# Queuing the attention of a chunk two slots later, and copying W's blocks out of PSUM one unit later, in a FAVOR attention and bilinear FFN kernel on Trainium2

## The chip, the cores and the metric

The kernel runs on one core of one Trainium2 chip. Its time is the device time of one execution in microseconds (us), and lower is better. The kernel before took 929.81 us, the median of 3 runs (929.26 to 933.73).

## The reference, cut to what matters

All of it, with the shapes (q, k and v are [8, 8, 576, 64], omega is [128, 64], and the weights are float64):

```python
def phi(x):                                   # x is q or k, divided by 64 ** 0.25
    proj = einsum('bhsd,md->bhsm', x, omega)  # 128 features
    h = proj - sum(x * x, -1, keepdims=True) / 2
    h = h - max(h, -1, keepdims=True)
    return exp(h) / sqrt(128)

q_p, k_p = phi(q), phi(k)
kv  = einsum('bhsm,bhsd->bhmd', k_p, v)
z   = sum(k_p, axis=2)
num = einsum('bhsm,bhmd->bhsd', q_p, kv)
den = einsum('bhsm,bhm->bhs', q_p, z)[..., None] + 1e-06
x   = (num / den).transpose(0, 2, 1, 3).reshape(4608, 512)
out = ((x @ w1) * (x @ w2) @ w3) @ w_out      # w1, w2 [512, 1024], w3 [1024, 1024], w_out [1024, 512]
```

## The kernel before, in words

**The work.** The 4608 tokens are 36 chunks of 128. For each chunk of q and of k the kernel computes features; from k and v it makes kv and z for each of the 8 batches (a batch is 4.5 chunks); a chunk of q then attends, and its result x goes through the bilinear FFN. The last two matrices are multiplied once at the start (W = w3 w_out). Large products run in fp16, each operand as a high and a low part, three passes (PASSES, L25).

**The names.** They are the names of the program's tiles, and the profile's groups use them too.

- *Splits and features.* qraw and kraw are loaded by SyncE (SP); a norm (junk_q on ACT, then a small matmul in power_of_two, L155) gives a scale; qhl and khl are their two parts, the high one by ACT (L136), the low one by DVE (L139). qpj and kpj (L254) are the projections, 24 short matmuls on TensorE (PE) into a pair of PSUM banks; DVE takes the maximum nm (L259) and subtracts it (qe, L267); ACT takes the exponent (L268); eq and ek are the two parts of that, the high one by DVE or ACT (L125, L127), the low one mostly by POOL (L277).
- *Attention.* Two DMA transposes in SP's queue make eqT (L344). nu (L357, in q_attend) is the product with kv, 24 matmuls, into a pair of banks; DVE divides (xs). x_turn (called by ready) splits xs into xhl, and a DMA transposes it into xT (L398).
- *kvp* (L322) is the product of a batch's features with v, one per batch. vhl are the parts of v: of a batch five tiles, the low part of each by DVE at L139.
- *FFN.* A unit of gates (ab, L581) is 48 matmuls of 256 tokens into two single banks; ACT scales one (asb, L590), DVE multiplies with the other (L591), and POOL splits the product (arena, L595 and L596). Two chunks share four units. project_out (o, L607) is 24 matmuls on W for one chunk, an ACT copy and a store.
- *Weights.* Each block of float64 weights goes through from_float64: a fetch by a DMA of ACT's queue (L443), magnitude on ACT (L451) and four bit operations on DVE (bits, L457 to L461). For W a product follows: wp (L530), two single banks, which ACT copies (L535) or DVE adds (L537) into Wb.

**PSUM.** Two pairs of banks (pool ps_a) are used in turn by qpj, kpj, nu and kvp. Four single banks (ps_m) are used in turn by the small norms, wp, the gates, o and the sums of the weights (l1).

**What sets the order.** Each chunk has three slots (PACE). In step, every piece of a chunk is put into a slot with a rank: q's features at its first slot at0, q_attend at at0 + 2, ready at at0 + 3, the k chunk five chunks ahead. The main loop (L748) takes the slots in turn: first some ticks of the weights (PER; a tick holds one stage each of several blocks, set apart by SKEW, L44), then one unit from a queue of gates and project_outs (unit, L637), then the planned pieces by rank. After slot 40 unit leaves two in the queue (RESERVE). A scheduler then orders the instructions of each engine, near to this order but not always in it; an engine runs its own in order, and waits for others by semaphores.

What the change touches: SKEW (L44), features (L245), from_float64's list (L467), W_block (L519), the padding of units (L662), and the two lines of step for q_attend and ready (L724, L725).

Of the kernel before, what the change touches and what calls it, by code (L numbers as in the profile page):

```python
# [7 lines left out]

F32 = mybir.dt.float32
# [4 lines left out]
AF = mybir.ActivationFunctionType  # L14
# [4 lines left out]
P = 128  # L19
# [5 lines left out]
PASSES = ((0, 0), (0, 1), (1, 0))  # L25
# [13 lines left out]
DQ = "10"  # L39
DK = "11111110"  # L40


ORDER = "ooWWWW11a22booWWWW11a22bS"
SKEW = [0, 1, 2, 2, 3]  # L44

PER = [3, 1, 0, 1, 0, 1, 1, 0, 1, 0, 1, 1, 0, 1, 1, 0, 1, 1, 1, 1, 1] + 12 * [1]
PACE = {}
GROUPS = [(0, 1), (1, 1), (2, 1), (3, 1)]
RESERVE = 2
EAGER = 40  # L50
RAW64_BUFS = 3
O_BUFS = 3
RAW_BUFS = 2
# [10 lines left out]
def tile_favor_attention_then_bilinear_ffn(  # L64
# [19 lines left out]
    nc = tc.nc  # L84
    NCH = qT.shape[0]
    H, D = v.shape[2], v.shape[3]
    HD = H * D
    NP = H // 2
    M = omT.shape[1]
# [17 lines left out]
    def banks(name):  # L107
        return ps_a.tile([P, 2, 512], F32, tag="pa", name=name)
# [4 lines left out]
    def small(name, n=1, rows=P, dt=F32, bufs=4):  # L113
        return sm.tile([rows, n], dt, tag=f"s_{name}", name=name, bufs=bufs)

    ones_bf = const.tile([P, P], BF16, name="ones_bf")
    nc.vector.memset(ones_bf, 1.0)
    ones = const.tile([P, P], F32, name="ones")
# [10 lines left out]
    def pick(kinds, i):  # L129
        return kinds[min(i, len(kinds) - 1)]  # L130
# [114 lines left out]
    def features(c, name):  # L245


        hl, es = hls.pop((name, c))
        pj = banks(f"{name}pj_{c}").rearrange("p g (i m) -> p g i m", m=M)
        for i in range(NP):  # L250
            for n, (x, y) in enumerate(PASSES):
                for g in range(2):
                    d = slice(g * D, (g + 1) * D)
                    nc.tensor.matmul(  # L254
                        pj[:, g, i], hl[d, x, i], om[d, y], start=n == 0, stop=n == len(PASSES) - 1
                    )
        pj = pj.rearrange("p g i m -> p (g i) m")
        nm = small("nm", H)
        nc.vector.tensor_reduce(nm, pj, AX.X, ALU.max, negate=True)  # L259
        e = at.tile([P, H, M], F32, tag="e", name=f"{name}e_{c}", bufs=2)  # L260
        if pick(DK if name == "k" else DQ, c) == "1":

            nc.vector.tensor_scalar(nm, nm, es, 15 * math.log(2.0), ALU.mult, ALU.add)
            for h in range(H):
                nc.scalar.activation(e[:, h], pj[:, h], AF.Exp, scale=es, bias=nm[:, h : h + 1])
        else:
            nc.vector.tensor_tensor(e, pj, nm.unsqueeze(2).broadcast_to([P, H, M]), ALU.add)  # L267
            nc.scalar.activation(e, e, AF.Exp, scale=es, bias=ln_e)  # L268
        return e
# [76 lines left out]
    def q_attend(c):  # L346

        t = eqs.pop(c)
        owners = [
            (b, max(b * S - c * P, 0), min((b + 1) * S - c * P, P))  # L350
            for b in range(c * P // S, ((c + 1) * P - 1) // S + 1)
        ]
        nu = banks(f"nu_{c}")[:, :, 0 : 4 * E].rearrange("p g (i e) -> p g i e", e=E)
        for h in range(H):
            for b, r0, r1 in owners:
                for n, (x, y) in enumerate(PASSES):
                    nc.tensor.matmul(  # L357
                        nu[r0:r1, h // 4, h % 4],
                        t[:, x, place(h), r0:r1],
                        kvs[b][:, y, h],  # L360
                        start=n == 0,
                        stop=n == 2,
                    )

        gd = small("gd", H)
        nc.vector.tensor_scalar_add(
            gd.rearrange("p (g i) -> p g i", g=2), nu[:, :, :, D], 1e-6 * M * 2.0**21
        )
        gr = small("gr", H)
        nc.vector.reciprocal(gr, gd)  # L370
        xs = at.tile([P, HD], F32, tag="xs", name=f"xs_{c}", bufs=1)
        nc.vector.tensor_tensor(
            xs.rearrange("p (g i d) -> p g i d", g=2, d=D),
            nu[:, :, :, 0:D],
            gr.rearrange("p (g i) -> p g i", g=2).unsqueeze(3).broadcast_to([P, 2, 4, D]),
            ALU.mult,
        )
        mx = small("mx")
        nc.vector.tensor_reduce(mx, xs, AX.X, ALU.max, apply_absolute_value=True)
        xss[c] = xs, mx, owners  # L380
# [54 lines left out]
    def from_float64(new, src, name):  # L435

        st = {}

        def fetch():
            at = st["at"] = raw_at.pop(0)  # L440
            raw = arena[:, at : at + 4].bitcast(U32).rearrange("p b i -> p (b i)")

            nc.scalar.dma_start(raw.rearrange("p (j i) -> p j i", j=src.shape[1]), src)  # L443
            st["raw"] = raw.rearrange("p (i t) -> p i t", t=2)

        def magnitude():

            at = st["mag"] = mag_at.pop(0)
            st["g"] = arena[:, at : at + 2].rearrange("p b i -> p (b i)")
            st["dst"] = new()  # L450
            nc.scalar.activation(st["g"], st["raw"][:, :, 1].bitcast(F32), AF.Abs)  # L451

        def bits():
            g = st["g"]
            top, low = st["raw"][:, :, 1], st["raw"][:, :, 0]

            nc.vector.tensor_scalar(g, g, F64_TOP, F64_LEAST, ALU.min, ALU.max)  # L457
            g = g.bitcast(U32)
            nc.vector.tensor_scalar(g, g, 3, 0x3FFFFFFF, ALU.logical_shift_left, ALU.bitwise_and)
            nc.vector.scalar_tensor_tensor(g, top, 0xC0000000, g, ALU.bitwise_and, ALU.bitwise_or)  # L460
            nc.vector.scalar_tensor_tensor(  # L461
                st["dst"].bitcast(U32), low, 29, g, ALU.logical_shift_right, ALU.bitwise_or
            )
            raw_at.append(st["at"])
            mag_at.append(st["mag"])

        return [fetch, magnitude, bits, lambda: None]  # L467

    l1s = {}
    done = set()  # L470
# [48 lines left out]
    def W_block(n):  # L519

        i, j0 = n * 2 % NF, n * 2 // NF * HALF
        at = HALF + n % 2 * 2
        w3c = guest[:, at : at + 2].rearrange("p b i -> p (b i)")

        def product():
            w = w3c.rearrange("p (j i) -> p j i", j=HALF)
            for k in range(2):
                ps = bank_m(f"wp_{n}_{k}")
                for j in range(HALF):
                    nc.tensor.matmul(  # L530
                        ps, w[:, j, k * P : (k + 1) * P], guest[:, j], start=j == 0, stop=j == HALF - 1
                    )
                Wi = Wb[:, i + k + 1]
                if j0 == 0:
                    nc.scalar.copy(Wi, ps)  # L535
                else:
                    nc.vector.tensor_tensor(Wi, ps, Wi, ALU.add)  # L537
                    square_sum(wam[:, i + k : i + k + 1], Wi, f"W{i + k}")

        src = w3T[j0 * P : (j0 + HALF) * P, 2 * i * P : 2 * (i + 2) * P]  # L540
        return from_float64(lambda: w3c, src.rearrange("(j p) i -> p j i", p=P), f"w3_{n}") + [product]

    def W_split():
        p, s = power_of_two(wam, NF, "W", add=True, bufs=1)
# [113 lines left out]
    for ch in ORDER:  # L658
        n = seen.get(ch, 0)
        seen[ch] = n + 1  # L660
        st = make[ch](n)
        units.append([None] * 4 + st if len(st) == 1 else st + [None] * (5 - len(st)))  # L662
    behind = sorted(range(5), key=lambda k: -SKEW[k])
    ticks = [
        [units[t - SKEW[k]][k] for k in behind if 0 <= t - SKEW[k] < len(units) and units[t - SKEW[k]][k]]
# [17 lines left out]
    def put(slot, rank, fn):  # L683
        plan.setdefault(slot, []).append((rank, len(plan[slot]) if slot in plan else 0, fn))
# [19 lines left out]
    def step(i):  # L704
        at0 = begin[i]
        kc = i + LEAD
        keys = [(n, c) for n, c in (("q", i), ("k", kc)) if 0 <= c < NCH]
        state = {}

        def norms():  # L710
            state["am"] = norm(keys, i)

        def splits():
            for name, c in keys:
                split_raw(c, name)
                if c + 2 < NCH:
                    load(srcs[name], c + 2, name)

        put(at0 - 3, 3, norms)
        put(at0 - 2, 6, lambda: scale(keys, state["am"]))  # L720
        put(at0 - 1, 8, splits)
        if i >= 0:
            put(at0, 1, lambda: q_chunk(i))
            put(at0 + 2, 7, lambda: q_attend(i))  # L724
            put(at0 + 3, 0, lambda: ready(i))  # L725
        if kc < NCH:
            put(at0, 2, lambda: k_chunk(kc))
        if kc in B_OF_K:

            def kv():  # L730
                v_unit(len(v_work))
                kv_batch(B_OF_K[kc])

            put((begin[i + 1] if i + 1 in begin else at0 + 3) - 1, 5, kv)
        for b in range(B):
            cs = [c for c, _, _ in chunks_of(b)]
            if cs[1] == kc:
                put(at0, 9, lambda b=b: v_batch(b))
            if cs[0] == kc:
                put(at0 + 2, 10, lambda cs=cs: [v_load(c) for c in cs if c not in vraw])  # L740
# [59 lines left out]
```

## Time and profile before

| | before |
|---|---|
| median of 3 runs | 929.81 us |
| the profiled execution | 932.87 us |
| its span, first to last instruction | 931.1 us |
| mean granted clock of TensorE | 0.929 |
| busy: PE | 809.9 us (87%) |
| busy: DVE | 637.7 us (68%) |
| busy: ACT | 406.9 us (44%) |
| busy: POOL | 324.7 us (35%) |

The profile shows one execution. Busy time is a share of the span. A group of the profile reads "line, engine, operation, out<-in"; "<-DMA eqT<-eq" behind idle time says what ended it. The rows of busy tenths cut the span into 40 slices of 23.3 us; PEclk is the clock that PE was granted, in tenths. The first of the 36 chunks of q begins (its first qpj) at 94.6 us, chunk 8 at 285.4 us and the last at 857.8 us; before the first one lie loading, the first k chunks and the first part of the weights.

### The profile page before, as it was taken

To read this page: it belongs to the slowest core of one execution; us is meant where nothing else is said; L and a number is where in the kernel's file an instruction comes from. 1 tells how busy PE (TensorE), PEld (TensorE's weight loads), DVE (VectorE), ACT (ScalarE), POOL (GpSimd) and SP (SyncE) were. 2 spreads that over 40 slices of the span, in tenths; PEclk is the share of its full clock that TensorE was granted. 3 is DMA by queue.
4 is the path that set the end of the run, shared out by engine and by line. 5 is a ranking of instruction groups with operands and counts; after the bars stand their busy time and mean duration, and the time that the engine had idled before them with its cause. 6 is when DMAs were issued, how large, how long until landed. Compare 5 with 4: busy or idle time off the path is not lost.

```text
span 931.1 us, 20482 instructions
## 1 busy us (share of the span) xinstructions
PE 809.9 (87%) x8593; PEld 598.3 (64%) x8598; DVE 637.7 (68%) x1119; ACT 406.9 (44%) x695; POOL 324.7 (35%) x317
## 2 busy tenths in 40 slices
PE   1964397689996998999989998989899989999998
PEld 1433253577775766777757766767577757777774
DVE  5779789889787478667876787566857875556210
ACT  3587764556435343444344533444354333322111
POOL 0000004232454256433543464343533643423311
PEclk9985599689998799999989998999899989999999
DMA  8445455332444145333432343243423422333200
GB/s 312 163 137 181 136 148 178 83 70 59 92 114 83 43 91 126 92 70 81 114 80 69 80 125 80 65 96 79 115 71 69 69 59 58 74 76 58 46 24 34
DMA packets 142524, 88.42 MB, mean 95 GB/s; under 512 B 116704, under 2 KB 116832, under 8 KB 142432
## 3 DMA queue, kind: packets, MB, share of 16 engines
q1 hardware_dynamic: 134944, 66.15, 30.1%
q10 hardware_dynamic: 7488, 20.97, 6.7%
q8 instruction: 67, 1.10, 0.5%
q14 instruction: 25, 0.20, 0.1%
HBM read 49.35 MB, written 9.44 MB: 63 GB/s over the span
## 4 chain that ended last, share of the span: by engine, by line
PE 45%; DVE 25%; ACT 11%; DMA 10%; issue 5%; POOL 4%; ACTq 0%; DVEq 0%; SPq 0%; another core or an unknown queue 0%; POOLq 0%
PE ab L581 24%; PE o L607 9%; DVE nm L259 5%; PE kvp L322 4%; PE wp L530 4%; DMA eqT<-eq 3%; DMA qraw<-qT 3%; DVE qhl L139 3%; DVE vhl L139 2%; DVE qe L267 2%; POOL eq L277 2%; PE nu L357 2%; DVE ke L267 2%; ACT ke L268 1%; DMA xT<-xhl 1%
## 5 line engine op out<-in xcount | busy, mean ns | idle before, releaser
L581 PE MATMUL ab<-xT,w12b 128*128 128x256 f16 (+1 forms) x3840 | 408.7, 268 | 12.8 <-DMA xT<-xhl 11.4
L581 PEld LDWEIGHTS <-w12b 128*128 128x128 f16 x3840 | 351.4, 101 | 59.4 <-DMA xT<-xhl 6.8
L607 PE MATMUL o<-Wb,arena 128*128 128x512 f16 x864 | 194.4, 379 | 1.3 <-DVE Wb L139 0.8
L595 POOL TENSOR_SCALAR arena<-asb 128x512 f16<-128x512 f32 x72 | 59.7, 829 | 256.4 <-DVE asb L591 249.5
L607 PEld LDWEIGHTS <-arena 128*128 128x128 f16 x864 | 84.4, 100 | 93.9 <-issue 1.4
L277 POOL TENSOR_TENSOR eq<-qe,eq 128x1024 f16<-128x1024 f32 x34 | 73.3, 2157 | 139.7 <-DVE eq L125 139.7
L268 ACT ACTIVATE qe<-qe,ln_e,es 128x1024 f32<-128x1024 f32 x35 | 43.4, 1240 | 149.5 <-DVE qe L267 149.5
L596 POOL TENSOR_TENSOR arena<-asb,arena 128x512 f16<-128x512 f32 x72 | 92.0, 1277 | 6.0
L139 DVE SCALAR_TENSOR_TENSOR qhl<-qraw,s,qhl 128x512 f16<-128x512 f32 x36 | 68.5, 1904 | 28.6 <-ACT qhl L136 28.5
L591 DVE TENSOR_TENSOR asb<-ab,asb 128x512 f32<-128x512 f32 x72 | 49.5, 688 | 55.3 <-PE ab L581 54.9
L277 POOL TENSOR_TENSOR ek<-ke,ek 128x1024 f16<-128x1024 f32 x28 | 61.5, 2195 | 46.6 <-DVE ek L125 45.3
L153 ACT ACTIVATE junk_q<-qraw 128x512 bf16<-128x512 f32 x36 | 22.7, 631 | 125.2 <-DMA qraw<-qT 125.2
L357 PE MATMUL nu<-kv,eqT 128*128 128x65 f16 (+1 forms) x960 | 40.7, 204 | 40.5 <-DMA eqT<-eq 40.0
L357 PEld LDWEIGHTS <-eqT 128*128 128x128 f16 (+1 forms) x960 | 35.6, 107 | 51.6 <-DMA eqT<-eq 45.2
L530 PE MATMUL wp<-w12b 128*128 128x512 f32 x128 | 62.4, 644 | 4.8 <-DVE w12b L461 4.8
L322 PE MATMUL kvp<-vhl,ek 128*128 128x65 f16 x960 | 50.5, 206 | 11.0 <-POOL ek L277 4.7
L603 DVE TENSOR_SCALAR osc<-pt,kap 128x1 f32<-128x1 f32 x36 | 9.6, 272 | 68.8 <-ACT o L611 68.7
L322 PEld LDWEIGHTS <-ek 128*128 128x128 f16 x960 | 41.4, 104 | 22.4 <-POOL ek L277 4.8
L590 ACT ACTIVATE asb<-ab 128x512 f32<-128x512 f32 x72 | 41.8, 580 | 28.2 <-PE ab L581 28.2
L254 PE MATMUL kpj<-om,khl 64*128 64x128 f16 x864 | 34.0, 226 | 21.5 <-ACT khl L136 17.2
L530 PEld LDWEIGHTS wp<-w12b 128*128 128x128 f32 x128 | 25.7, 206 | 35.6 <-issue 29.9
L393 ACT ACTIVATE xhl<-xs,p2r 128x512 f16<-128x512 f32 x36 | 25.8, 718 | 49.3 <-DVE p2r L182 44.3
(120 smaller groups left out, 1037.5 us busy)
## 6 DMA issues: line engine op xcount, KB each, us to landing
kraw<-kT SPq DMA_DIRECT2D x36, 256.0 KB, 3.0
vraw<-v SPq DMA_DIRECT2D x36, 256.0 KB, 3.0
qraw<-qT SPq DMA_DIRECT2D x36, 256.0 KB, 2.6
out<-o SPq DMA_DIRECT2D x36, 256.0 KB, 2.0
arena<-w3T ACTq DMA_DIRECT2D x8, 1024.0 KB, 5.4
arena<-w ACTq DMA_DIRECT2D x8, 1024.0 KB, 5.9
arena<-wo ACTq DMA_DIRECT2D x4, 1024.0 KB, 5.3
eqT<-eq SPq DMA_TRANSPOSE x72, 3.0
```

The source lines that it names most:

```text
L139: nc.vector.scalar_tensor_tensor(lo, src, s, hi, ALU.mult, ALU.subtract)
L259: nc.vector.tensor_reduce(nm, pj, AX.X, ALU.max, negate=True)
L268: nc.scalar.activation(e, e, AF.Exp, scale=es, bias=ln_e)
L277: (nc.vector if lo == "d" else nc.gpsimd).tensor_tensor(t[:, 1], e, t[:, 0], ALU.subtract)
L322: nc.tensor.matmul(ps[:, h // 4, h % 4], ek[c][r0:r1, x, place(h)], vhl[c][r0:r1, y, h], start=n == 0, stop=n == len(mm) - 1,)
L357: nc.tensor.matmul(nu[r0:r1, h // 4, h % 4], t[:, x, place(h), r0:r1], kvs[b][:, y, h], start=n == 0, stop=n == 2,)
L530: nc.tensor.matmul(ps, w[:, j, k * P : (k + 1) * P], guest[:, j], start=j == 0, stop=j == HALF - 1)
L581: nc.tensor.matmul(ps[:, k], w12[m][i][cc][:, a, r * P : (r + 1) * P], x[:, b, cc, off : off + T], start=j == 0, stop=j == len(mm) - 1,)
L591: nc.vector.tensor_tensor(asb, ab[1], asb, ALU.mult)
L595: nc.gpsimd.tensor_scalar(h[:, 0], asb, 1.0, 1.0, ALU.mult, ALU.mult)
L596: nc.gpsimd.tensor_tensor(h[:, 1], asb, h[:, 0], ALU.subtract)
L607: nc.tensor.matmul(ps, hs[c, f][0][:, a], W[f][:, b], start=i == 0, stop=i == len(mm) - 1)
```

## The change

It has three parts.

- *The attention.* From chunk 8 on (EARLY; the ninth chunk) q_attend is put at at0 + 4 and ready at at0 + 5, before at0 + 2 and at0 + 3. Chunks 0 to 7 stay as they were.
- *W.* What came behind wp's matmuls in product (the copy or the add into Wb, and the square sum) is now a stage of its own, keep, one unit later: W_block has five stages, from_float64 three (an empty one is gone), and SKEW puts the fourth three units and the fifth four units behind the first. The magnitudes and splits of w1 and w2 stay in their ticks; there is one tick more at the end.
- *The identity.* A tile ident (made by POOL) and a third kind of features, "2", which subtracts the maximum by a matmul with it. No chunk has that kind: DQ and DK are as before.

```diff
-SKEW = [0, 1, 2, 2, 3]
+SKEW = [0, 1, 2, 3, 4]
...
+EARLY = 8
...
+    ident = const.tile([P, P], F32, name="ident")
+    make_identity(nc, ident)
...
+        project()
         nm = small("nm", H)
...
-        if pick(DK if name == "k" else DQ, c) == "1":
+        kind = pick(DK if name == "k" else DQ, c)
+        if kind == "2":
+
+            project(lambda h: nm[:, h : h + 1].broadcast_to([P, M]))
+            nc.scalar.activation(e, pj, AF.Exp, scale=es, bias=ln_e)
+        elif kind == "1":
...
-        return [fetch, magnitude, bits, lambda: None]
+        return [fetch, magnitude, bits]
...
+        pss = []
 
         def product():
...
+                pss.append(ps)
+
+        def keep():
+            for k, ps in enumerate(pss):
                 Wi = Wb[:, i + k + 1]
                 if j0 == 0:
                     nc.scalar.copy(Wi, ps)
...
-        return from_float64(lambda: w3c, src.rearrange("(j p) i -> p j i", p=P), f"w3_{n}") + [product]
+        return from_float64(lambda: w3c, src.rearrange("(j p) i -> p j i", p=P), f"w3_{n}") + [
+            product,
+            keep,
+        ]
...
-        units.append([None] * 4 + st if len(st) == 1 else st + [None] * (5 - len(st)))
+        units.append([None] * 3 + st + [None] if len(st) == 1 else st + [None] * (5 - len(st)))
...
-            put(at0 + 2, 7, lambda: q_attend(i))
-            put(at0 + 3, 0, lambda: ready(i))
+            lag = 2 if i < EARLY else 4
+            put(at0 + lag, 7, lambda: q_attend(i))
+            put(at0 + lag + 1, 0, lambda: ready(i))
```

In the fences below a row is an engine's instruction: line, operation, out<-in with the buffers' own numbers, tile. Lines shift between the two kernels (L254 is now L264, L357 is L377, L581 is L609, L607 is L635, L535 is L560).

On PE, chunk 16 up to the projection of chunk 17; each row is the first of a group of matmuls, and the rest of its group is left out. Before:

```order
L254 MATMUL kpj_21_6008<-om_82,khl_21_5891 128x128
...
L581 MATMUL ab_12_3_1_6075<-xT_6_5087,w12b_104 128x256
...
L607 MATMUL o_11_6120<-Wb_105,arena_107 128x512
...
L357 MATMUL nu_16_6148<-kv_3_4855,eqT_16_6005 128x65
...
L581 MATMUL ab_14_0_0_6196<-xT_7_5681,w12b_104 128x256
...
L254 MATMUL qpj_17_6263<-om_82,qhl_17_6181 128x128
```

The same place on PE after the change:

```order
L264 MATMUL kpj_21_5884<-om_87,khl_21_5778 128x128
...
L635 MATMUL o_10_5928<-Wb_110,arena_112 128x512
...
L377 MATMUL nu_15_5964<-kv_3_4775,eqT_15_5591 128x65
...
L609 MATMUL ab_12_2_0_6002<-xT_6_5173,w12b_109 128x256
...
L609 MATMUL ab_12_3_0_6083<-xT_6_5173,w12b_109 128x256
...
L264 MATMUL qpj_17_6138<-om_87,qhl_17_6068 128x128
```

In the stretch of chunk 16 there now stands the attention of chunk 15, behind an o and ahead of both units of gates, where that of chunk 16 stood before; units and project_outs of the queue come later by about one chunk's share. Where the lag changes, the stretch of chunk 10 has one unit of gates and no o, and the missing pieces run behind the projection of chunk 35. Behind nu of chunk 35 both orders are alike.

On DVE, from the splits of v (vhl) to the features of chunk 16. Before:

```order
L139 SCALAR_TENSOR_TENSOR vhl_18_6045<-vraw_18_5322,s1_3_5902,vhl_18_6045 128x8x64
L394 SCALAR_TENSOR_TENSOR xhl_15_5968<-xs_15_5882,p2r1_4_5964,xhl_15_5968 128x512
L139 SCALAR_TENSOR_TENSOR vhl_19_6113<-vraw_19_5324,s1_3_5902,vhl_19_6113 128x8x64
L139 SCALAR_TENSOR_TENSOR vhl_20_6191<-vraw_20_5326,s1_3_5902,vhl_20_6191 128x8x64
L139 SCALAR_TENSOR_TENSOR vhl_21_6336<-vraw_21_5328,s1_3_5902,vhl_21_6336 128x8x64
L591 TENSOR_TENSOR asb_12_2_5956<-ab_12_2_1_5931,asb_12_2_5956 128x512
L139 SCALAR_TENSOR_TENSOR vhl_22_6404<-vraw_22_5330,s1_3_5902,vhl_22_6404 64x8x64
L259 TENSOR_REDUCE nm_5997<-qpj_16_5972 128x8
L267 TENSOR_TENSOR qe_16_5999<-qpj_16_5972,nm_5997 128x1024
```

The same place on DVE after the change:

```order
L143 SCALAR_TENSOR_TENSOR vhl_18_5921<-vraw_18_5185,s1_3_5789,vhl_18_5921 128x8x64
L143 SCALAR_TENSOR_TENSOR vhl_19_5997<-vraw_19_5187,s1_3_5789,vhl_19_5997 128x8x64
L143 SCALAR_TENSOR_TENSOR vhl_20_6078<-vraw_20_5189,s1_3_5789,vhl_20_6078 128x8x64
L143 SCALAR_TENSOR_TENSOR vhl_21_6211<-vraw_21_5191,s1_3_5789,vhl_21_6211 128x8x64
L143 SCALAR_TENSOR_TENSOR vhl_22_6287<-vraw_22_5193,s1_3_5789,vhl_22_6287 64x8x64
L619 TENSOR_TENSOR asb_12_1_5843<-ab_12_1_1_5818,asb_12_1_5843 128x512
L274 TENSOR_REDUCE nm_5873<-qpj_16_5848 128x8
L287 TENSOR_TENSOR qe_16_5875<-qpj_16_5848,nm_5873 128x1024
```

xhl of the chunk before no longer stands among the splits of v; these still stand ahead of nm and qe.

On ACT, around the first two copies of W. Before:

```order
L265 ACTIVATE ke_0_176<-kpj_0_149,nm_174,es_136 128x128 x8
L535 COPY Wb_105<-wp_0_0_199 128x512
L127 CAST ek_0_186<-ke_0_176 128x1024
L535 COPY Wb_105<-wp_0_1_205 128x512
L451 ACTIVATE arena_107<-arena_107 128x1024
L136 ACTIVATE khl_1_217<-kraw_1_111,s3_4_195 128x512
```

The same place on ACT after the change:

```order
L285 ACTIVATE ke_0_181<-kpj_0_154,nm_179,es_141 128x128 x8
L471 ACTIVATE arena_112<-arena_112 128x1024
L131 CAST ek_0_191<-ke_0_181 128x1024
L140 ACTIVATE khl_1_220<-kraw_1_116,s3_4_200 128x512
L560 COPY Wb_110<-wp_0_0_204 128x512
L560 COPY Wb_110<-wp_0_1_209 128x512
```

The magnitude of the next block and the high part of k's second chunk now stand ahead of both copies.

More of the change, by code (lines that the diff above doesn't have):

```diff
@@ L6 @@
 from concourse import mybir
+from concourse.masks import make_identity
 from concourse._compat import with_exitstack
@@ L248, in features, with project @@
         hl, es = hls.pop((name, c))
[L249 to L257, printed above, removed]
+        pg = banks(f"{name}pj_{c}").rearrange("p g (i m) -> p g i m", m=M)
+        pj = pg.rearrange("p g i m -> p (g i) m")
+        def project(first=None):
+            for i in range(NP):
+                if first is not None:
+                    for g in range(2):
+                        nc.tensor.matmul(pg[:, g, i], ident, first(g * NP + i), start=True, stop=False)
+                for n, (x, y) in enumerate(PASSES):
+                    for g in range(2):
+                        d = slice(g * D, (g + 1) * D)
+                        nc.tensor.matmul(
+                            pg[:, g, i],
+                            hl[d, x, i],
+                            om[d, y],
+                            start=first is None and n == 0,
+                            stop=n == len(PASSES) - 1,
+                        )
+        project()
         nm = small("nm", H)
```

## The prediction

> **What bounds the kernel now.** I read the page first, then TensorE's waits, then stretches of single chunks, then the instructions of two chunks in order of time. The page says that TensorE (PE) is the busiest engine, and that its clock is at times not granted in full.
>
> ```profile
> span 931.1 us, 20482 instructions
> PE 809.9 (87%) x8593; PEld 598.3 (64%) x8598; DVE 637.7 (68%) x1119; ACT 406.9 (44%) x695; POOL 324.7 (35%) x317
> PEclk9985599689998799999989998999899989999999
> ```
>
> From 319 us to 858 us (qpj of chunk 9 to qpj of chunk 35) PE waits for one thing alone. The row of the waits gives the total, the number and the longest:
>
> ```profile
> PE nu L357 <- DMA eqT<-eq: 26.3, 15, 2.7
> ```
>
> So the attention of a chunk (nu) comes to the head of PE's queue before the transposed features eqT have landed. The stretches below each run from the qpj of one chunk to the next (chunks 9, 10, 11, 12, 16, 18, 23, 29, 31), and the last over all 26. Columns: length, then busy time of PE, PEld, DVE, ACT, POOL, then PE's granted clock.
>
> ```profile
> 319.00:337.10 18.10, 18.10 (x197) 13.89 (x196) 13.25 (x23) 8.18 (x13) 8.49 (x6) 1.00 0.36 88
> 337.10:356.20 19.10, 18.46 (x197) 14.13 (x196) 14.83 (x31) 8.54 (x14) 9.96 (x8) 1.00 0.40 84
> 356.20:379.80 23.60, 19.75 (x197) 14.79 (x198) 18.72 (x28) 8.69 (x14) 12.68 (x10) 0.93 0.50 124
> 379.80:403.20 23.40, 23.40 (x317) 18.22 (x318) 14.71 (x24) 11.16 (x20) 9.12 (x16) 1.00 0.32 69
> 459.00:484.30 25.30, 20.88 (x195) 15.38 (x194) 19.24 (x29) 11.30 (x21) 12.60 (x10) 0.87 0.40 105
> 507.70:525.80 18.10, 18.10 (x195) 13.87 (x194) 13.25 (x22) 7.90 (x12) 8.49 (x6) 1.00 0.41 88
> 612.70:635.00 22.30, 19.88 (x195) 14.85 (x194) 14.74 (x26) 9.73 (x15) 8.48 (x6) 0.92 0.35 81
> 738.80:764.20 25.40, 20.96 (x197) 15.40 (x198) 19.19 (x29) 8.31 (x13) 13.25 (x10) 0.87 0.24 53
> 805.30:822.70 17.40, 17.40 (x173) 13.19 (x174) 9.58 (x20) 4.77 (x8) 5.65 (x5) 1.00 0.35 78
> 319.00:857.80 538.80, 512.22 (x5631) 389.74 (x5630) 372.74 (x646) 219.30 (x352) 239.42 (x213) 0.97 0.35 82
> ```
>
> An undisturbed chunk is 18.1 us of PE without a hole, 5.3 more (23.4) with the product kvp of a batch, and 17.4 once the k chunks are done (31 to 34). The five chunks in which DVE splits a batch of v (11, 16, 20, 25, 29; I call them split chunks) have 5 to 6 us more DVE work (19.24 against 13.25) and last 23.6 to 25.4. All 26 undisturbed would take 22 x 18.1 + 4 x 17.4 + 5 x 5.3 = 494.3; some 1.7 more for five small norms and three chunks with double the nu matmuls, 496. The stretch takes 538.8, so 42.8 us are lost: 26.6 idle, and 16 in which PE ran slower. That is what the change can win here.
>
> An ordinary chunk (12), and then chunk 16, in order of time:
>
> ```profile
> 403.17 0.84 PE L254 MATMUL qpj<-om,qhl 64*128 64x128 f16 x24
> 404.06 1.23 DVE L259 TENSOR_REDUCE nm<-qpj 128x8 f32<-128x1024 f32 x1
> 405.39 1.23 DVE L267 TENSOR_TENSOR qe<-qpj,nm 128x1024 f32<-128x1024 f32 x1
> 409.75 2.14 POOL L277 TENSOR_TENSOR eq<-qe,eq 128x1024 f16<-128x1024 f32 x1 [3.77 <-DVE eq L125]
> 410.01 5.34 PE L607 MATMUL o<-Wb,arena 128*128 128x512 f16 x24
> 415.28 0.96 PE L357 MATMUL nu<-kv,eqT 128*64 128x65 f16 x48
> ```
>
> ```profile
> 459.02 0.84 PE L254 MATMUL qpj<-om,qhl 64*128 64x128 f16 x24
> 460.46 5.42 PE L581 MATMUL ab<-xT,w12b 128*128 128x256 f16 x48
> 460.95 2.94 DVE L139 SCALAR_TENSOR_TENSOR vhl<-vraw,s,vhl 128x512 f16<-128x512 f32 x3
> 465.07 1.21 DVE L259 TENSOR_REDUCE nm<-qpj 128x8 f32<-128x1024 f32 x1
> 466.31 1.23 DVE L267 TENSOR_TENSOR qe<-qpj,nm 128x1024 f32<-128x1024 f32 x1
> 470.60 2.13 POOL L277 TENSOR_TENSOR eq<-qe,eq 128x1024 f16<-128x1024 f32 x1 [3.74 <-DVE eq L125]
> 473.68 0.24 PE L357 MATMUL nu<-kv,eqT 128*128 128x65 f16 x2 [2.48 <-DMA eqT<-eq]
> 475.85 1.39 PE L357 MATMUL nu<-kv,eqT 128*128 128x65 f16 x22 [1.94 <-DMA eqT<-eq]
> ```
>
> The two transposes of each chunk stand among the page's DMA issues, with the median time to landing:
>
> ```profile
> eqT<-eq SPq DMA_TRANSPOSE x72, 3.0
> ```
>
> In chunk 12 POOL ends eq at 411.9 and a transpose takes 3.0, so eqT lands at about 414.9; PE arrives at 415.3, 0.4 us later. In chunk 16 nm starts 6.05 us behind qpj and not 0.9, because it stands behind the splits of v; eqT is there only at 475.85, and PE waits twice, 2.48 and 1.94. Then the clock is halved for a while (0.87 over the chunk), so 4.4 us of waiting cost 7.2.
>
> **The change part by part: the attention.** From chunk 9 on PE now meets the nu of chunk i-1 behind qpj(i), kpj and one o, which is 1.45 + 5.2 + 0.15 = 6.8 us behind qpj(i) (460.46 - 459.02 for the first part, o's 5.34 less its overlap). Counted from its own qpj that is 18.1 + 6.8 = 24.9; eqT was there after 16.8 in the worst chunk (475.85 - 459.02). 8 us are to spare, so this wait goes everywhere, and the slow matmuls behind it with it. In chunks 9 and 12 to 34 that is 42.8 less the loss of chunks 10 and 11 ((19.1 - 18.3) + (23.6 - 18.1) = 6.3): **36.5 us**.
>
> What is late next? nu(i-1) takes the pair of PSUM banks that qpj(i) had, as the pairs are used in turn, and the last reader of that is qe(i) on DVE. In an ordinary chunk qe ends 3.45 us behind qpj (405.39 + 1.23 - 403.17), and nu asks at 6.8: no wait. In a split chunk qe ended 8.5 behind qpj (466.31 + 1.23 - 459.02), and that would be a wait of 1.7. With PE no longer halted in the chunk before, bounds come from DVE's work: it starts on a chunk 0.9 behind qpj and has 19.24 to do before the next nm, and nm and qe take 2.5. Without idle time the pair is free at 22.6, and with the 4.85 of idle time of an ordinary chunk (18.10 - 13.25) at 27.5; PE asks at 18.4 + 6.8 = 25.2. So 0 to 2.3 us each. Some of the idle time stays (xhl and the splits wait for ACT and POOL), so I take 0.8, for four chunks **-3.2** (0 to -9.2).
>
> Where the lag changes, the queue runs down to its reserve for two slots: chunk 10 has one unit of gates and no o, 10.6 us of PE work less (5.3 + 5.3), which is done behind qpj_35 instead. Chunks 10 and 11 then leave PE 42.7 - 6.3 - 10.6 = 25.8 us of work, and DVE 14.83 + 18.72 = 33.55. PE needs of that what comes before q's split for chunk 12, all but the last 3 us or so; I take 30.4. With the moved work that is 41.0 against 42.7: **+1.7** (+6.3 if nothing waits, -1.5 if all 33.55 are waited out). DVE is then late into chunk 12, for its qe and for the ek of kvp: **-1.4** (0 to -3).
>
> The tail costs nothing: behind nu_35 both orders are the same, four half gates, o_31 and so on, and xT has 16 us (two units of 5.3 and an o) to land, as before. The SP queue keeps its loads; each xT transpose stands one chunk later, behind the raw loads of its slot, and nobody asks for it sooner.
>
> **The change part by part: W and the identity.** The engines that wait for W's products, and what PE waits for in the same stretch (0 to 215 us); then 120 to 190 us:
>
> ```profile
> ACT Wb L535 <- PE wp L530: 7.4, 4, 2.4
> DVE Wb L537 <- PE wp L530: 2.2, 1, 2.2
> PE wp L530 <- DVE w12b L461: 4.8, 3, 3.0
> PE ab L581 <- DMA xT<-xhl: 11.4, 3, 6.5
> PE kpj L254 <- DVE kv L332: 2.3, 1, 2.3
> 120.00:190.00 70.00, 50.21 (x477) 33.14 (x478) 63.38 (x100) 37.82 (x71) 17.96 (x12) 0.84 0.50 135
> ```
>
> ACT and DVE no longer stand in front of an unfinished product, 9.6 us of waiting at most. But up to 58 us PE works at wp itself, and later DVE is the busy one (63 of 70 us), with PE waiting for the xT that it makes. So I count **+2** (from -5, two waits as that of kpj for kv, to +9.6). A product's two banks are held one unit longer; PE's waits before include none for a copy of W. [...]
>
> The identity is used by no chunk, and adds a memset and a select on POOL, which is idle then:
>
> ```profile
> POOL 0000004232454256433543464343533643423311
> ```
>
> The select isn't in the trace. From 0.2 us (as the other memsets) to 2.2 (a POOL operation on eight times the elements, above), inside some 140 us without POOL work: 0, and without that cover 2.
>
> **Sum.** 36.5 - 3.2 + 1.7 - 1.4 + 2 = 35.6. The profiled execution took 932.87 (span 931.1 and 1.8 around it); 897.3 there. The median shown is 929.81, 3.06 below it, so I forecast **894**.
>
> **The rivals.** *The wait only moves to the PSUM pair.* All four later split chunks wait 2.3 us, and slow down as chunk 16 did (7.2 for 4.4, so 3.8 each, 15); chunks 10 to 12 lose 4.5 and W wins nothing: 36.5 - 15 - 4.5 = 17, 913. For it: nm stands behind the splits as it did. Against: DVE has 18 us per chunk for 13 of work. [...]
>
> *Held banks stop PE.* The four banks that W's products, gates and norms share run out in each of the eight products, for 2.3 us as in the kpj row: 18, and without the +2: 33.6 - 18 = 15, 914. Against: PE never waited for such a copy.
>
> *Slower.* qe(i) is late in every chunk and not in five, as DVE now works at qhl, xs and the gates of two chunks at once. It decides from 36.5 / 26 = 1.4 us of wait per chunk, that is with qe 8.2 behind qpj. As late as in chunk 16 everywhere it costs 26 x 1.7 = 44 for the 36.5 won: 937. Against: 4.85 us of idle DVE in each ordinary chunk.
>
> *It does nothing,* if the scheduler put nu where it stood: the order of the instructions shows it moved. 930.
>
> **How the numbers follow.** Forecast 0.78 (its own ends: all terms at their best 36.5 + 6.3 + 9.6 = 52, 877; at their worst 36.5 - 9.2 - 1.5 - 3 - 5 = 18, 912), PSUM pair 0.13, held banks 0.05, slower 0.03, nothing 0.01. Within 0.5% (4.6 us) a measurement of this kernel can't tell a difference from none. Faster by more than that: the first three less their tails, 0.93; same 0.03; slower 0.04. The range 880 to 913 leaves out the thin end of the forecast and about half of the two rivals near 913.
>
> **What would show it.** Right: no wait of nu for eqT from chunk 8 on, split chunks of 18 to 20 us, a clock of 1.00 from chunk 13 to the end, PE idle under 1 us there outside chunks 10 to 12. Wrong: nu waiting for qe in ordinary chunks, chunks of over 19 us without a kvp, or wp waiting for a copy of W before 160 us.

## The result, and the profile after

The changed kernel took 907.53 us (median of 4 runs, 904.3 to 908.24), against 931.77 of the kernel before beside it: a ratio of 0.9734, with a 95% interval of 0.9694 to 0.9774. It is faster by 24 us; 36 were forecast. The profiled execution took 904.3 (span 902.5), the lowest of the four.

In the rows below line numbers are those of the changed kernel: nu is L377, qe L287, qpj and kpj L264, the gates L609, o L635, the splits L143. The head of the page:

```profile
span 902.5 us, 20479 instructions
PE 798.6 (88%) x8592; PEld 597.2 (66%) x8598; DVE 604.9 (67%) x1119; ACT 408.4 (45%) x695; POOL 306.2 (34%) x319
PEclk9975599668998799999999999999999999999999
```

From the fifteenth slice on every digit of the clock is a 9; before, four of these were an 8. What PE waits for from chunk 9 to the last projection (total, number and longest):

```profile
PE nu L377 <- DVE qe L287: 7.3, 7, 1.8
PE kpj L264 <- DVE p2p L183: 1.7, 1, 1.7
PE kvp L342 <- POOL ek L297: 1.2, 2, 0.6
PE qpj L264 <- DVE qhl L143: 0.5, 1, 0.5
```

The waits of nu for eqT (26.3 us) are gone from here. In their place stand 7.3 us of nu waiting for qe, the reader of the PSUM pair. The stretches of chunks 10, 11, 12, 16, 17 and 20, and all 26 from chunk 9 to 34 (columns as in the prediction):

```profile
338.50:347.10 8.60, 8.18 (x125) 7.08 (x125) 8.14 (x15) 3.87 (x4) 3.75 (x3) 1.00 0.11 21
347.10:367.70 20.60, 18.44 (x195) 13.97 (x195) 20.22 (x40) 9.57 (x16) 13.50 (x11) 1.00 0.64 161
367.70:391.10 23.40, 23.40 (x315) 18.31 (x315) 14.53 (x26) 13.15 (x26) 9.95 (x18) 1.00 0.42 101
445.70:464.90 19.20, 18.23 (x195) 14.05 (x194) 16.52 (x28) 7.26 (x10) 9.58 (x8) 1.00 0.49 124
464.90:491.00 26.10, 23.73 (x315) 18.58 (x314) 13.12 (x25) 14.00 (x27) 9.87 (x16) 1.00 0.36 73
527.30:546.90 19.60, 18.25 (x195) 14.05 (x195) 16.33 (x28) 7.27 (x10) 9.95 (x8) 1.00 0.53 135
320.50:818.10 497.60, 486.93 (x5561) 377.09 (x5560) 339.12 (x644) 220.09 (x350) 218.29 (x211) 1.00 0.39 88
```

Chunks 16 and 20, two of the split chunks, last 19.2 and 19.6 us in place of 25.3 and 25.4, and PE is no longer slowed in them. Chunk 17, a kvp chunk, is 2.7 over its 23.4. Here are chunk 16 and then chunk 17 in order of time, on PE, ACT and DVE:

```profile
445.37 5.12 DVE L143 SCALAR_TENSOR_TENSOR vhl<-vraw,s,vhl 128x512 f16<-128x512 f32 x5 [1.93 <-POOL vhl L142]
445.74 0.84 PE L264 MATMUL qpj<-om,qhl 64*128 64x128 f16 x24
451.02 1.21 DVE L274 TENSOR_REDUCE nm<-qpj 128x8 f32<-128x1024 f32 x1
452.26 1.23 DVE L287 TENSOR_TENSOR qe<-qpj,nm 128x1024 f32<-128x1024 f32 x1
453.63 0.90 PE L377 MATMUL nu<-kv,eqT 128*128 128x65 f16 x24 [0.97 <-DVE qe L287]
...
466.70 0.63 ACT L157 ACTIVATE junk_k<-kraw 128x512 bf16<-128x512 f32 x1 [2.06 <-DMA kraw<-kT]
469.71 0.58 ACT L618 ACTIVATE asb<-ab 128x512 f32<-128x512 f32 x1
470.32 0.69 DVE L619 TENSOR_TENSOR asb<-ab,asb 128x512 f32<-128x512 f32 x1 [5.15 <-ACT asb L618]
470.93 1.22 DVE L274 TENSOR_REDUCE nm<-qpj 128x8 f32<-128x1024 f32 x1
473.62 0.89 PE L377 MATMUL nu<-kv,eqT 128*128 128x65 f16 x24 [1.76 <-DVE qe L287]
```

In chunk 16 nm stands behind five splits of v, as before, and qe ends 7.7 us behind qpj where nu asked at 6.9. In chunk 17 no split is near: there asb stands ahead of nm on DVE, and waits 5.15 us for ACT, which has the norm of k, waiting for kraw, and three norms of v ahead of it.

### The profile page after: what moved, and what is told of

Its sections match the earlier page's. It is cut to its first block, busy times and chain, and to the rows that moved or that the text cites. A ratio compares the mean times of both kernels' runs of the same rounds, so it can differ in the third digit from the quotient of the medians.

```text
span 902.5 us, 20479 instructions
## 1 busy us (share of the span) xinstructions
PE 798.6 (88%) x8592; PEld 597.2 (66%) x8598; DVE 604.9 (67%) x1119; ACT 408.4 (45%) x695; POOL 306.2 (34%) x319
## 4 chain that ended last, share of the span: by engine, by line
PE 58%; DVE 22%; ACT 7%; issue 5%; DMA 4%; POOL 3%; ACTq 0%; SPq 0%; DVEq 0%; POOLq 0%
PE ab L609 30%; PE o L635 14%; PE kvp L342 5%; DVE nm L274 4%; PE wp L551 3%; DVE vhl L143 3%; DVE qe L287 2%; PE nu L377 2%; DMA kraw<-kT 2%; DVE arena L480 2%; DVE asb L619 2%; PE qpj L264 1%; DVE ke L287 1%; PE kpj L264 1%; ACT ke L288 1%
## 5 line engine op out<-in xcount | busy, mean ns | idle before, releaser
L609 PE MATMUL ab<-xT,w12b 128*128 128x256 f16 (+1 forms) x3840 | 398.6, 266 | 9.2 <-DMA xT<-xhl 9.2
L609 PEld LDWEIGHTS <-w12b 128*128 128x128 f16 x3840 | 349.6, 100 | 49.7 <-DMA xT<-xhl 5.9
L635 PE MATMUL o<-Wb,arena 128*128 128x512 f16 x864 | 195.5, 380 | 2.6 <-DVE Wb L143 1.8
L635 PEld LDWEIGHTS <-arena 128*128 128x128 f16 x864 | 82.1, 98 | 96.8 <-issue 1.9
L623 POOL TENSOR_SCALAR arena<-asb 128x512 f16<-128x512 f32 x72 | 47.6, 661 | 286.4 <-DVE asb L619 252.1
L624 POOL TENSOR_TENSOR arena<-asb,arena 128x512 f16<-128x512 f32 x72 | 85.5, 1187 | 6.0
L342 PE MATMUL kvp<-vhl,ek 128*128 128x65 f16 x960 | 53.2, 211 | 13.3 <-POOL ek L297 6.3
L377 PE MATMUL nu<-kv,eqT 128*128 128x65 f16 (+1 forms) x960 | 35.7, 200 | 21.9 <-DMA eqT<-eq 14.5
L377 PEld LDWEIGHTS <-eqT 128*128 128x128 f16 (+1 forms) x960 | 33.1, 106 | 26.0 <-DMA eqT<-eq 15.8
L143 DVE SCALAR_TENSOR_TENSOR qhl<-qraw,s,qhl 128x512 f16<-128x512 f32 x36 | 46.0, 1278 | 6.3 <-ACT qhl L140 6.1
L288 ACT ACTIVATE ke<-ke,ln_e,es 128x1024 f32<-128x1024 f32 x29 | 36.0, 1240 | 30.9 <-DVE ke L287 29.5
L264 PE MATMUL kpj<-om,khl 64*128 64x128 f16 x864 | 33.8, 227 | 16.7 <-ACT khl L140 11.5
L274 DVE TENSOR_REDUCE nm<-kpj 128x8 f32<-128x1024 f32 x36 | 43.7, 1215 | 3.4 <-PE kpj L264 3.3
```

Of the source, the lines that this page charges most:

```text
L143: nc.vector.scalar_tensor_tensor(lo, src, s, hi, ALU.mult, ALU.subtract)
L264: nc.tensor.matmul(pg[:, g, i], hl[d, x, i], om[d, y], start=first is None and n == 0, stop=n == len(PASSES) - 1,)
L342: nc.tensor.matmul(ps[:, h // 4, h % 4], ek[c][r0:r1, x, place(h)], vhl[c][r0:r1, y, h], start=n == 0, stop=n == len(mm) - 1,)
L377: nc.tensor.matmul(nu[r0:r1, h // 4, h % 4], t[:, x, place(h), r0:r1], kvs[b][:, y, h], start=n == 0, stop=n == 2,)
L609: nc.tensor.matmul(ps[:, k], w12[m][i][cc][:, a, r * P : (r + 1) * P], x[:, b, cc, off : off + T], start=j == 0, stop=j == len(mm) - 1,)
L624: nc.gpsimd.tensor_tensor(h[:, 1], asb, h[:, 0], ALU.subtract)
```

## The experiments

**The two parts of the change, each alone.** The first kernel has the new lag and the old weights:

```diff
-SKEW = [0, 1, 2, 3, 4]
+SKEW = [0, 1, 2, 2, 3]
-        return [fetch, magnitude, bits]
+        return [fetch, magnitude, bits, lambda: None]
...
-            product,
-            keep,
+            product,
```

> The attention two slots later from chunk 8 on, with the weights as in the kernel before (the identity is kept). Theory: the lag alone removes nu's waits for eqT and the halved clock behind them, and W's part is worth nothing, because DVE sets the time up to chunk 4 with or without it: ratio to before 0.974 (0.970 to 0.978, some 908 us), nu's waits for eqT behind chunk 9 zero, qpj of chunk 4 within 2 us of the 207 that both kernels have. Rival: the W part brings a part of the 24 us (the 8 us by which chunk 3 started earlier): 0.980 to 0.983. Other rival: W's part costs the 1.5 us by which chunk 9 starts later after the change: 0.972.

Measured: 903.1 us, ratio 0.969 (0.9664 to 0.9716). From chunk 9 on nu waited for eqT nowhere, and 7.8 us for qe. Chunk 4 began at 204.3, 2.7 us before the 207 of the other two kernels where I had expected 2 at most, and the ratio lies under the range that I gave (0.970 to 0.978). So the lag alone brings all of the gain; and it was, if anything, faster than the whole change. The identity stays in this kernel and in all that follow, so its term of 0 isn't tested by itself.

The second has the new weights and a lag of two slots throughout:

```diff
-EARLY = 8
+EARLY = 36
```

> The W part and the identity alone; every attention stays at two slots. Theory: W's part is worth nothing: ratio to before 0.998 to 1.002, nu waiting for eqT 35 to 42 us in all as before, chunk 3 begins some 8 us sooner and chunk 4 at 207 again. Rival (the sooner start is kept): 0.991 to 0.994. Rival (banks held longer stop PE): 1.002 to 1.005.

Measured: 930.3 us, ratio 0.9986 (0.9967 to 1.0006), nu waiting for eqT 42.9 us. Chunk 3 began at 169.3, 7.9 us sooner than before, and chunk 4 at 207.0. The sooner start is given back within chunk 3. The stretch of chunk 3 in the kernel before, and in the changed one:

```profile
177.20:207.10 29.90, 22.34 (x349) 19.51 (x350) 27.82 (x52) 15.71 (x27) 7.11 (x14) 0.71 0.30 72
```

```profile
169.20:206.90 37.70, 25.32 (x349) 22.68 (x351) 32.83 (x61) 17.58 (x31) 8.39 (x15) 0.64 0.27 65
```

PE has the same matmuls (x349); DVE has 52 instructions and 27.82 us there before, 61 and 32.83 after. The DVE work that PE had run ahead of was still to be done.

**The change once more,** beside the next two experiments on one chip:

> The changed kernel once more, timed in one go with the next two, to hold against the attention alone (0.969). If W's part is worth nothing, 0.969 as well (0.966 to 0.972), and the median of 907.5 was on the high side; if W's part costs PE the later start of chunk 9, 0.973.

Measured: 907.26 us, ratio 0.9716 (0.9684 to 0.9748). All ten runs of the change have a median of 907.5. The interval overlaps that of the attention alone; the ninth experiment decides between them.

**Where nu stands: three slots, five slots.**

```diff
-            lag = 2 if i < EARLY else 4
+            lag = 2 if i < EARLY else 3
```

> Three slots instead of four from chunk 8 on. nu then stands behind qpj, kpj and 10 matmuls of a gate unit, 2.55 us behind qpj. If eqT alone mattered, it is as good as four slots, 0.974, since eqT (16.8 us behind its qpj at worst) is there at 20.6. By the theory of the PSUM pair nu asks before qe of the next chunk has left the pair (3.45 us behind qpj in an ordinary chunk, 8.5 in a split chunk): 0.9 us of wait in some 20 chunks and 6 in the four split chunks, 18 + 24, less the 7.3 of the change: 0.974 + 35/930 = 1.01 (1.00 to 1.02), with nu waiting for qe 35 to 45 us and a clock halved again behind the waits of 6 us.

Measured: 944.86 us, ratio 1.0138 (1.0101 to 1.0175), 1.4% slower than before, as the theory of the PSUM pair had it. What PE waits for from chunk 10 on, the stretches of an ordinary chunk (13) and of chunk 16, and chunk 13 in order of time:

```profile
PE nu L377 <- DVE qe L287: 36.1, 20, 5.1
```

```profile
401.70:421.00 19.30, 18.30 (x197) 13.83 (x197) 13.26 (x23) 9.49 (x16) 8.22 (x6) 1.00 0.35 83
459.90:483.70 23.80, 20.06 (x196) 14.91 (x194) 17.21 (x28) 9.03 (x14) 10.98 (x9) 0.93 0.50 112
```

```profile
401.75 0.84 PE L264 MATMUL qpj<-om,qhl 64*128 64x128 f16 x24
404.08 1.23 DVE L287 TENSOR_TENSOR qe<-qpj,nm 128x1024 f32<-128x1024 f32 x1
405.45 0.89 PE L377 MATMUL nu<-kv,eqT 128*128 128x65 f16 x24 [0.99 <-DVE qe L287]
```

eqT had landed long before, and nu still waited 0.99 us in this ordinary chunk, until qe was read out of the pair (404.08 + 1.23 = 405.31). So the second condition of nu, the PSUM pair, is as real as the first.

```diff
-            lag = 2 if i < EARLY else 4
+            lag = 2 if i < EARLY else 5
```

> Five slots instead of four. nu then stands behind qpj, kpj, one gate unit and one o, 12 us behind qpj. By the theory of the PSUM pair qe (at most 9 us behind qpj) is always done: nu's 7.3 us of waits for qe go, and nothing else changes but 5.3 us of PE work that moves behind the last projection: 7 us less than the change, ratio 0.966 (0.963 to 0.970). If those waits only hide others (DVE as the bound in split chunks, kvp waiting for ek): 0.973 to 0.976.

Measured: 932.86 us, ratio 1.0008 (0.9985 to 1.0032): no gain at all, and no theory of mine had that. The waits for qe did go (0.4 us left), but others came. What PE waits for from chunk 9 on, and chunk 17 in order of time:

```profile
PE kpj L264 <- DVE xs L392: 12.0, 5, 3.8
PE kpj L264 <- ACT junk_k L157: 3.6, 1, 3.6
```

```profile
472.44 0.84 PE L264 MATMUL qpj<-om,qhl 64*128 64x128 f16 x24
474.66 0.63 ACT L157 ACTIVATE junk_q<-qraw 128x512 bf16<-128x512 f32 x1 [4.50 <-DMA qraw<-qT]
475.29 0.67 ACT L639 ACTIVATE o<-o,osc 128x512 f32<-128x512 f32 x1
475.99 0.27 DVE L631 TENSOR_SCALAR osc<-pt,kap 128x1 f32<-128x1 f32 x1 [2.65 <-ACT o L639]
476.18 0.68 DVE L392 TENSOR_TENSOR xs<-nu,gr 128x512 f32<-128x512 f32 x1
477.01 1.46 PE L264 MATMUL kpj<-om,khl 64*128 64x128 f16 x24 [3.73 <-DVE xs L392]
```

nu now has one unit of gates behind it before the next projections, not two, and kpj takes the pair that nu had. xs, the last reader of nu, stands on DVE behind osc, which waits for ACT's copy of o, which stands behind a norm that waits for a load. So there is a third condition, on the other side: xs must be done before the next kpj. Of the places tried, four slots comes nearest to meeting all three.

**What is left of the waits.** In the sixth kernel (attention alone) three of five tiles of v in a batch go to POOL and ACT; "m" is POOL and DVE, "p" POOL and ACT:

```diff
-VS = "aaaaam"
+VS = "aaaaa" + "mpmpp" * 7
```

> The attention alone as in the first experiment, and of each batch from the second on only two of the five tiles of v are split on DVE; the other three are scaled and subtracted by POOL and copied by ACT, so that DVE has 3 splits less (3.1 us) ahead of nm in a split chunk. Theory: what is left of nu's waits for qe in chunks 16, 20, 25 and 29 (0.97, 1.35, 0.97 and 1.34 in the changed kernel) comes from these splits and goes, so 4.6 us less than the attention alone: ratio 0.964 (0.962 to 0.967); the waits of chunks 17 and 26 (1.76 and 0.48) stay, since there asb stands ahead of nm on DVE and waits for ACT's norms of v. Rival: POOL and ACT, with three more operations each, become late themselves: eq or the arena is later, PE waits for those, and the ratio is 0.969 or above.

Measured: 897.93 us, ratio 0.9625 (0.9598 to 0.9652). Chunks 16 and 17:

```profile
446.60:464.70 18.10, 18.10 (x197) 13.98 (x198) 14.46 (x25) 9.77 (x15) 12.90 (x12) 1.00 0.48 133
464.70:488.90 24.20, 23.59 (x317) 18.52 (x318) 12.85 (x24) 13.86 (x27) 9.31 (x16) 1.00 0.40 77
```

The split chunk is an undisturbed one now (18.1), so its wait came from the splits. The waits of nu in chunks 17 and 26, which I had expected to stay, went too.

The tenth kernel makes the same edit to the splits, but with a lag of two slots throughout and the old weights:

> The attention at two slots throughout, the weights as in the kernel before; only the v splits are shared with POOL and ACT. By my theory the large waits of nu for eqT come from the five splits ahead of nm in a split chunk: with three less, nm, eq and eqT come 3.1 us sooner, PE's 4.4 us of waiting there (2.48 and 1.94) shrink to 1.3 in each of five chunks, and no clock is halved behind them. Of some 7 us lost per split chunk 1.5 stay: 5 x 5.5 = 27 less, ratio 0.971 (0.968 to 0.978). If the lag is needed (eqT is late in any chunk): 0.99 or above.

Measured: 915.23 us, ratio 0.9817 (0.9795 to 0.9838), between the two ratios that I had named (0.971, and 0.99 or above). The waits from chunk 9 on, and chunk 16:

```profile
PE nu L377 <- DMA eqT<-eq: 17.6, 14, 2.0
```

```profile
457.09 0.84 PE L264 MATMUL qpj<-om,qhl 64*128 64x128 f16 x24
460.48 1.21 DVE L274 TENSOR_REDUCE nm<-qpj 128x8 f32<-128x1024 f32 x1
469.33 0.24 PE L377 MATMUL nu<-kv,eqT 128*128 128x65 f16 x2
471.50 0.85 PE L377 MATMUL nu<-kv,eqT 128*128 128x65 f16 x22 [1.94 <-DMA eqT<-eq]
```

nm starts 3.4 us behind qpj in place of 6.05, and the first wait (2.48) is gone. The second isn't: eqT comes by two transposes, and in chunk 16 before nu's two waits for them ended 2.17 us apart (473.68 and 475.85); of these the later one is there here too, 1.94 us. The five split chunks last 107.6 us together in place of 125.0, which is all of the gain; the rest, and the small waits of ordinary chunks, need the lag.

**Where the lag begins.** The seventh kernel is the attention alone with

```diff
-EARLY = 8
+EARLY = 7
```

> The attention alone, but two slots later from chunk 7 on and not from 8. By the theory nu of chunk 7 no longer waits (4.6 us in the changed kernel, and a halved clock behind it, some 3 us more): 7 us less, 0.962. Against it: chunk 8 then has two units of gates less before kvp of the third batch, which needs ek of chunk 13; that is ready some 14 us behind its projection, and PE has 5.3 + 2.7 us of gates until then, so it waits 5 us longer than the 5.1 of the change, and the gain is 2 at most: 0.967 to 0.971.

Measured: 898.23 us, ratio 0.9616 (0.9581 to 0.9651). The full 7 us, but not for the reason that I gave. nu of chunk 7 no longer waits for eqT (4.32 us in the attention alone), yet PE stands as long in the same place: 4.79 us for qhl, before the projection of chunk 8. What goes is behind that. kvp of the third batch waited 2.8 us in two pieces (1.55 and 1.21) for the 4.37 of the attention alone, as it now starts among gate units and not behind them; the clock is 1.00 from 297.3 to 322.3, and its last 104 matmuls take 4.78 us. In the changed kernel kvp waited 5.08 there, the clock was 0.50 from 303.6 to 317.3, and the last 106 took 7.57. From the projection of chunk 7 to that of chunk 12 the two profiles show 89.7 us for 94.8. So what I had held against this kernel didn't come either.

**Both together, with and without W's part.** The eighth has both edits on the attention alone; the ninth is the changed kernel with both, so that only W's part lies between them.

> The attention two slots later from chunk 7 on, the v splits shared as in the sixth experiment, the weights as in the kernel before. If the two savings are separate (nu of chunk 7; nu behind the split chunks), they add: 0.962 less 0.0065 = 0.955 (0.952 to 0.958). If both only fill the same hole in front of kvp of the third batch: 0.960 to 0.962.

> The eighth experiment's kernel with the W part of the change added; the two differ in nothing else and run on the same chip. If W's part is worth nothing, both have the same ratio within 0.002. If it costs what the change and the attention alone differ by (907 against 903): 0.004 above the other. If the sooner start of chunk 3 is kept: 0.004 to 0.008 below.

Measured: 888.38 us, ratio 0.9535 (0.9521 to 0.9549), without W's part; 893.07 us, 0.9588 (0.9567 to 0.9608), with it. The two savings add. The eighth is the fastest kernel of this study: 4.6% below the kernel before and 2% below the change. And W's part costs some 0.5% beside the lag. Without the lag, in the second experiment, it cost nothing that shows (0.9967 to 1.0006); why the two differ is open.

The profiled execution of the ninth was the fastest of its five, so both were profiled once more:

> The ninth experiment's kernel once more, for a second profile: the profiled execution of the ninth was the fastest of its five (888.02; the others 891 to 896), so that its trace doesn't show what W's part costs. Expected some 893 us. If W's part costs in the weights' stretch, the 5 us stand before chunk 9 (qpj of chunk 9 at 297 to 300 and not 295.2); if the cost is the phase of the clock's grid, a halved stretch stands somewhere that the eighth experiment's trace hasn't.

> The eighth experiment's kernel once more, for a second profile beside that of the eleventh: 888 to 890 us and qpj of chunk 9 within 1 us of 295.2, as the eighth's runs lay within 1.7 us.

Measured, one run of each: 892.66 with W's part, 888.6 without. Stretches of chunk 4, of chunk 5 and of chunks 6 to 8, without W's part and then with it:

```profile
209.00:236.20 27.20, 23.95 (x357) 18.94 (x355) 22.47 (x53) 16.95 (x30) 7.22 (x5) 0.94 0.28 55
236.20:256.10 19.90, 19.53 (x297) 15.74 (x297) 15.45 (x26) 8.83 (x16) 8.25 (x6) 1.00 0.37 87
256.10:295.50 39.40, 35.26 (x415) 26.10 (x414) 34.19 (x59) 20.96 (x34) 23.12 (x19) 1.00 0.46 115
```

```profile
210.10:237.60 27.50, 23.04 (x350) 18.45 (x349) 21.01 (x49) 14.78 (x27) 6.89 (x5) 0.94 0.22 50
237.60:259.40 21.80, 20.60 (x298) 15.96 (x296) 15.71 (x27) 9.88 (x17) 8.25 (x6) 1.00 0.42 86
259.40:299.70 40.30, 36.74 (x418) 27.23 (x418) 34.59 (x59) 21.07 (x34) 23.09 (x19) 0.96 0.44 113
```

From chunk 9 to chunk 34 both take the same time, 506.9 and 506.8 us. The 4.2 us stand ahead of it (299.7 less 295.5): 1.1 up to chunk 4, 0.3 and 1.9 in chunks 4 and 5, where PE has 2 us more idle time, and 0.9 in chunks 6 to 8, with a clock halved once (0.96). So both causes that I had named for the eleventh run are seen, the weights' stretch with the larger part. Why PE waits more in chunks 4 and 5 with W's part is left open.

## Why the prediction was right, and where it was short

The direction and the mechanism were right, and 907.5 is in the range of 880 to 913. The forecast of 894 was 13.5 too low. By its own terms, in the profiled executions (931.1 to 902.5, 28.6 us against 35.6):

- **Waits for eqT and the halved clock, 36.5: right.** In chunks 9 and 12 to 34 nu waits for eqT nowhere, and the clock is 1.00 over the 497.6 us. The first, second and third experiments show that it is the place of nu that does it. The full clock isn't there in every execution: in the profile of the change once more (span 906.7) these 26 chunks took 500.8 us, and in chunk 17 the clock was 0.50 from 477.6 to 481.0, behind a wait of 2.37 us for DVE.
- **The wait moves to the pair in split chunks, -3.2: the mechanism was right, the size was short.** nu waited 0.97, 1.35, 0.97 and 1.34 there, 4.6 in all, within the bounds (0 to 9.2). The sixth experiment shows that these come from the splits.
- **DVE late into chunk 12, -1.4: it wasn't.** Chunk 12 lasted 23.4. But waits that I had not priced came instead: 1.76 and 0.48 in chunks 17 and 26, where ACT's norms hold asb and asb holds nm, and 1.2 of kvp for ek with 0.5 of qpj. That is the step that failed in the attention: I looked for what delays qe only on DVE, and left out what DVE itself waits for. In all, chunks 9 and 12 to 34 went from 496.1 to 468.4, 27.7 for the 31.9 forecast.
- **Chunks 10 and 11, +1.7:** 42.7 became 8.6 + 20.6 = 29.2, 13.5 less, for 10.6 us of moved work. The last stretch, from chunk 35 to the last matmul, grew by 11.2 (69.4 to 80.6), so +2.3.
- **W, +2: wrong in sign.** Chunk 9 began at 320.5 and not 319.0, so -1.5 in this execution, and the eighth and ninth experiments put it at -4.7 by their medians. That lies within my bounds (-5 to +9.6). ACT and DVE do stand less before unfinished products (6.3 us for 9.6), but the time is given back in chunk 3, where DVE is the busy engine. I had written that down, and counted +2 nevertheless. The rival of held banks isn't what happened: no product waits for a copy in any trace here.
- **The sum and the medians.** 27.7 + 2.3 - 1.5 = 28.5 is the 28.6 measured between the two profiled executions. I put the median 3.06 under the profiled execution, as before; after, the profiled execution was the lowest of four and the median 3.2 above it. This alone is 6.3 of the 13.5, and which execution was profiled is chance.

Of the rivals, the one with the PSUM pair came in part, at 1.0 to 1.4 us for 2.3, and without slow matmuls in the split chunks. Of my own signs of being wrong, two came in part: chunks 16, 20, 25 and 29 last 19.2 to 19.6 us without a kvp (which I had also called a sign of being right, 18 to 20), and PE stands idle for 1.1 to 2.4 us in each of chunks 17, 20, 26 and 29. The rival on the slower side is what happens one slot earlier: at three slots nu asks 2.7 us behind qpj, waits for qe in 20 chunks, and the kernel takes 945.

## What to carry to other kernels

An operation that shares a ring of buffers with its neighbours has a window and not only a due time: here nu must come behind its own input, behind the last reader of the pair before it, and early enough that its own reader is done before the next owner. Two, three and five slots each break one of the three; four meets all of them but for some 1 us in the split chunks and 1.8 and 0.5 us in chunks 17 and 26. Before a lag is priced, write down for each candidate slot who had the buffer, who takes it next, and what the engines of both readers wait for themselves.

## What the runs showed of the hardware

**A short wait can halve PE's clock, or not.** Two neighbouring stretches of 3.4 us in chunk 17, of the attention alone (after a wait of 2.22) and then of the changed kernel (1.76); the second column is PE's busy time, and the granted clock is third from the end:

```profile
468.40:471.80 3.40, 1.18 (x29) 1.11 (x28) 3.30 (x3) 1.02 (x1) 1.74 (x2) 1.00 0.01 2
471.80:475.20 3.40, 3.40 (x18) 2.34 (x17) 2.51 (x8) 2.15 (x3) 1.32 (x1) 0.50 0.06 12
```

```profile
470.90:474.30 3.40, 1.64 (x29) 1.29 (x28) 3.30 (x4) 0.79 (x1) 1.77 (x2) 1.00 0.01 2
474.30:477.70 3.40, 3.40 (x38) 3.06 (x35) 2.74 (x8) 2.15 (x3) 1.09 (x1) 1.00 0.02 5
```

In the traces before and after the change the halved stretches begin and end on a grid of 3.41 us and last one or more of its steps: 371.8 to 375.2 (before) is one, 303.6 to 317.3 (after) four. With PE busy 1.18 of a step the next was halved, with 1.64 it wasn't. The changed kernel showed both in chunk 17: in the profile of the change once more PE was busy 1.03 us from 474.2 to 477.6, and the clock was 0.50 in the 3.4 us behind. Of other steps at the full clock, one with PE busy 0.97 us (before, 624.4 to 627.8) and one with 1.47 (from chunk 7 on, in chunk 11, a single wait of 1.93) stood ahead of a halved one; two with 1.71 and 2.05 (after, 348.0 to 351.4 and 532.4 to 535.8) stood ahead of a full one. PE's busy time in one step doesn't settle it alone: with 1.41 in the kernel with three slots (487.1 to 490.5) the next step was full, and with 1.76 in the changed kernel (218.3 to 221.7) it was halved (0.51). That one kernel shows both may be a reason why its executions differ by a few us here; that was not tried by itself.

**The same DVE instruction costs 1.4 or 2.3 us by what POOL does beside it.** The low part of q, chunks of 400 to 800 us, before and after the change:

```profile
L139 DVE SCALAR_TENSOR_TENSOR qhl<-qraw,s,qhl 128x512 f16<-128x512 f32 x19 | 44.3, 2330 | 18.4 <-ACT qhl L136 18.4
```

```profile
L143 DVE SCALAR_TENSOR_TENSOR qhl<-qraw,s,qhl 128x512 f16<-128x512 f32 x21 | 28.9, 1377 | 1.4 <-ACT qhl L140 1.4
```

With the lag this split falls less on POOL's subtraction for ek: in chunk 16 before, that runs from 472.69 to 474.82 and qhl's split from 472.94 on, 2.43 us; after, from 458.64 to 460.77 and from 459.93 on, 1.39 us. Beside it run 18 of the 19 splits before and 18 of the 21 after; the other four took 0.75 us each. The split of k's low part beside it (khl, the same shape) runs clear of POOL's subtractions after the change and takes 0.73 us in the mean of these chunks. Altogether DVE has 604.9 us of work for 637.7 before. At three slots it is xhl's low part that takes longer (2.03 us for 0.75). None of this was in my sum.
